# Attention scores on tiles of 64 rows by 128 columns, one head each, in a transformer block on one core

## The chip, the cores and the metric

The kernel runs on one core of one Trainium2 chip. A core has TensorE (PE in the profile, its weight loads as PEld), VectorE (DVE), ScalarE (ACT), GpSimd (POOL) and SyncE (SP), which work at the same time and wait for one another by semaphores; each takes its instructions in a fixed order. On-chip memory for operands has 128 partitions; products land in a memory of their own, PSUM. The metric is the time on the device in microseconds, the median of several runs. Before the change it is 972.0 us in three runs (971.28, 972.0, 973.32).

## The reference

One block: an adaptive layer norm, sliding-window attention, a second adaptive layer norm and a gated feed-forward net. S = 2048 positions, D = 512, 32 heads of 16 numbers each, a window of 256 positions, F = 1792.

```
mod = (silu(c) @ w_mod).reshape(...)            # sa, ca, ga, sb, cb, gb
h = layernorm(x) * (1 + ca) + sa
q, k, v = (h @ wqkv) split into 32 heads of 16
scores = q k^T * 16**-0.5,  kept where 0 <= i - j < 256, else -1e9
x = x + ga * ((softmax(scores) @ v) @ wo)
h = layernorm(x) * (1 + cb) + sb
x = x + gb * ((silu(h @ w1) * (h @ w3)) @ w2)
```

All inputs and the output are float32. The products with high demands are made from parts: a number is split into a part of reduced precision (type fp32r) and the rest, and three products (high-high, high-low, low-high) are added up.

## The kernel before

**Units.** Attention is cut into 32 units, 8 groups of four heads (g) by 4 blocks of 512 positions (b). A unit is made in three stages that run on different units at the same time: `unit_a` makes the queries and keys of a group for a block (12 products `pj`, line 451, then copies by ScalarE, two subtractions by GpSimd and six DMAs into the tile `ring`); `unit_b` makes the maximum of each row of scores; `unit_c` makes the probabilities and the output. In a unit there are four blocks of 128 queries (qb) or keys (j), and the four heads are two pairs (a) of two heads (hh).

**The tile ring** holds queries and keys with 16 x 3 = 48 rows a head, since each number stands in three parts. Before the change it has three planes of 96 rows each: the queries of two heads one above the other (rows interleaved), and for each of the two heads a plane of keys in which the rows of the other head are zero. So one score product (line 504, tile `mx`, 96 rows) takes the queries of both heads, and the zero rows of the keys drop the other head. Four more rows (96 to 99) hold the row maxima, in two parts for each head, against rows of ones and zeros in the keys; the score products for the probabilities (line 763, tile `st`, 100 rows) so subtract the maximum. `ring_fill` writes zeros and ones with memsets on GpSimd, five for each block.

**unit_b** makes 16 products `mx` a unit, up to 384 keys each. `top` (line 511, VectorE) adds a mask and takes the maximum from PSUM, then `parts`, a transpose on TensorE (line 526, `turn`), a copy on ScalarE and two DMAs (`rows`, line 535) bring the maxima into ring.

**unit_c** makes 16 products `st` a unit and masks them in a mode that is given for each key block and pair of heads in the string `MODE` (last three units: `MODL`). C: VectorE merges two blocks under a predicate (line 781), ScalarE takes the exponential, GpSimd splits the result again (line 791). P: masking by GpSimd in a side tile. D: VectorE adds the mask in PSUM (line 771), then one exponential. E: TensorE adds the mask by a further product with the identity (line 766), then one exponential. The value products (`pv`, line 739) use tiles of 128 rows by 32 columns: four heads side by side, each product recorded as two passes, all into one bank `po`; line 828 copies the finished bank and a DMA (`store`) writes it to memory. A key block's probabilities are used by up to three query blocks, so the last two key blocks of a unit give a second product in the next unit ("carry").

**Order of the work.** In attention the order on every engine is written out: each step of a unit has a time in the table `X`, in units of an eighth of a unit's length, and all steps of all units are sorted by those times. `pj`, `mx` and `tl`, `st`, `c`, `pv`, `o` are the times of the projections, of the score products and their maxima, of the probability scores, of what follows them, of the value products and of the copy and store of the output. A second table, `Y`, orders the first units, which run among the value projection (line 671). From the time `TS` = 232 on (the last three units) the steps have fixed planned times, `us(t)` with the paces `TW`, and a planner deals the output projection (line 1120) and the start of the feed-forward net (lines 1384 and 1478) around them, by estimated costs. PSUM: three banks for `mx`, three for `st`, one for `pj`, one for `po`.

Of the kernel before, what the change touches and what calls it, by code (L numbers as in the profile page):

```python
# [12 lines left out]
ALU = mybir.AluOpType  # L13
# [16 lines left out]
X = dict(oa=-1.228, ob=1.317, wqk=(-2.382, 3.131, 4.551), pj=(-1.966, -1.918, -1.881, -0.877, -0.359, -0.355,  # L30
         -0.265, 0.076, 1.497, 3.335, 3.917, 4.363), ev=(4.727, 5.775, 5.259), mix=(5.588, 6.021),
         row=(8.681, 8.806, 9.018), mx=(0.546, 0.669, 1.455, 2.0, 2.064, 2.307, 2.929, 2.957, 3.255, 4.081,
         4.688, 5.039, 6.139, 6.215, 6.787, 7.106), tl=(0.31, 0.576, 0.39, 0.716, 0.354, 0.742, 0.497, 1.151,
         0.762, 0.785, 0.491, 0.953, 0.338, 1.726, 1.317, 1.105), mr=(8.575, 8.773, 9.063, 9.269), st=(1.873,
         1.594, -2.503, 2.891, 0.05, 3.409, 2.644, 3.504, 4.618, 4.477, 4.419, 5.916, 5.311, 7.665, 6.691,
         6.671), c=(0.385, 0.805, 2.402, 0.573, 0.759, 1.126), pv=(4.115, 8.948, 9.091, 9.582, 3.792, 4.101),
         o=(9.93, 10.63), job=(-0.855, 2.493, 10.058))
# [9 lines left out]
MODL = 'CECECECE'  # L47
# [223 lines left out]
TW = (243.0, 1.7, 1.5)  # L271
# [31 lines left out]
def block_kernel(ctx: ExitStack, tc: tile.TileContext, x, wqk, wv, wo, w13, w2, c, wmod, out):  # L303
# [13 lines left out]
    def fill_odd():  # L317

        for hh in range(2):
            r = slice(64 * hh, 64 * hh + 64)  # L320
            nc.vector.tensor_reduce(
                out=odd[r], in_=ident[r].rearrange("p (c o) -> p c o", o=4)[:, :, 2 - 2 * hh:4 - 2 * hh],
                op=ALU.add, axis=mybir.AxisListType.XY)
# [80 lines left out]
    mskk = mskw[:, :2]  # L404
    nc.gpsimd.memset(mskk, 0.0)
    WIN = (dict(pattern=[[1, P]], base=0, channel_multiplier=-1, compare_op=ALU.is_ge, fill=NEG),
           dict(pattern=[[-1, P]], base=0, channel_multiplier=1, compare_op=ALU.is_gt, fill=NEG))
    for j in range(2):
        nc.gpsimd.affine_select(out=mskk[:, j], in_=mskk[:, j], **WIN[j])
    later = ap.tile([P, P], mybir.dt.uint8, name="later")  # L410
    mskr = ap.tile([P, 2, P], F32R, name="mskr")
# [1202 lines left out]
```

## Time and profile before

| what | value |
|---|---|
| median of three runs | 972.0 us (971.28 to 973.32) |
| profiled execution, span | 971.3 us |
| instructions | 17150 |
| TensorE busy | 942.4 us, 97% |
| TensorE weight loads | 717.5 us, 74% |
| VectorE busy | 734.9 us, 76% |
| ScalarE busy | 557.1 us, 57% |
| GpSimd busy | 538.2 us, 55% |
| score products for maxima, line 504 | 512, 154.9 us busy |
| score products for probabilities, line 763 | 512, 155.3 us busy |
| value products, line 739 | 1408 passes, 98.6 us busy |

The span is one execution, from the first to the last instruction; the profiled execution's own time is this span. Busy times are unions: two instructions of one engine that overlap count once. A product is recorded with the pipeline's tail, so its recorded length is more than the time for which it holds the array; that time is read from start to start. Roughly, the first 45 us are loading and the first layer norm, up to 97 us the value projection with the first units in it, up to 445 us attention in steady state, up to 530 us the last units and the output projection, and then the feed-forward net, which the change doesn't touch.

### The profile page before, as it was taken

How to read it: one execution, taken by the hardware profiler on the slowest of the kernel's cores; microseconds unless marked ns; L12 is line 12 of the kernel's file. 1: busy time of each engine (PE TensorE's matmuls, PEld its weight loads, DVE VectorE, ACT ScalarE, POOL GpSimd, SP SyncE). 2: the span in 40 equal slices, each digit the busy share in tenths (PEclk: the TensorE clock that was granted, in tenths of full speed). 3: DMA queues.
4: the chain of work that ended last, by engine and by line, in shares of the span. 5: the costliest groups of instructions: out<-in, count | busy, mean ns of one | idle time of the engine just before them, and what ended most of it. 6: DMA issues, size and time to landing. Idle time of an engine off the chain costs nothing.

```text
span 971.3 us, 17150 instructions
## 1 busy us (share of the span) xinstructions
PE 942.4 (97%) x5316; PEld 717.5 (74%) x5316; DVE 734.9 (76%) x2034; ACT 557.1 (57%) x1258; POOL 538.2 (55%) x740
## 2 busy tenths in 40 slices
PE   6999999999999999998998999999999999999998
PEld 3678777777767776775577888888887888888886
DVE  7575889998989998999278686666679766677545
ACT  3333878787878787876578843433456343433330
POOL 8321777787868786865546765337759332222320
PEclk9999999999999999999898999999999999999999
DMA  9521354444544444435795564467654433222102
GB/s 317 170 77 36 134 182 143 144 143 144 176 143 143 144 144 143 133 128 174 211 243 139 194 217 151 142 206 249 194 195 165 141 119 94 63 65 72 44 23 87
DMA packets 80672, 141.65 MB, mean 146 GB/s; under 512 B 9538, under 2 KB 22338, under 8 KB 80580
## 3 DMA queue, kind: packets, MB, share of 16 engines
q1 hardware_dynamic: 79860, 139.50, 44.6%
q10 hardware_dynamic: 720, 1.05, 0.3%
q8 instruction: 42, 0.69, 0.3%
q14 instruction: 50, 0.41, 0.1%
HBM read 85.72 MB, written 34.61 MB: 124 GB/s over the span
## 4 chain that ended last, share of the span: by engine, by line
PE 83%; POOL 5%; DVE 4%; DMA 3%; issue 2%; ACT 2%; SPq 1%; POOLq 0%; DVEq 0%; ACTq 0%
PE st L1384 13%; PE mx L1384 11%; PE pj L451 7%; PE mx L504 7%; PE mx L1478 7%; PE st L763 7%; PE st L1478 7%; PE po L739 6%; PE pj L1384 5%; PE st L671 3%; PE pj L1478 2%; PE mx L1120 2%; POOL pt L791 2%; PE st L1120 2%; POOL qk L469 2%
## 5 line engine op out<-in xcount | busy, mean ns | idle before, releaser
L511 DVE CUSTOM_DVE_ANT_0 junk<-mx,mskq 128x384 bf16<-128x384 f32 (+2 forms) x512 | 256.3, 527 | 28.8 <-PE mx L504 27.2
L504 PE MATMUL mx<-ring 96*128 96x384 f32 (+2 forms) x512 | 154.9, 340 | 6.0 <-DMA ring<-qk 2.4
L763 PE MATMUL st<-ring 100*128 100x384 f32 (+2 forms) x512 | 155.3, 345 | 2.2 <-ACT pt L784 1.2
L791 POOL TENSOR_SCALAR_AFFINE_SELECT pt<-pt 128x256 f32<-128x256 f32 x268 | 109.3, 411 | 63.1 <-ACT pt L784 52.5
L451 PE MATMUL pj<-hT,wq 128*128 128x512 f32 x384 | 136.2, 404 | 1.2 <-DVE wq L440 0.8
L504 PEld LDWEIGHTS mx<-ring 96*128 96x128 f32 x512 | 93.5, 189 | 39.7 <-DVE mt L511 25.8
L784 ACT ACTIVATE pt<-st 128x256 f32<-128x256 f32 x268 | 96.1, 386 | 41.8 <-DVE st L781 33.8
L763 PEld LDWEIGHTS st<-ring 100*128 100x128 f32 x512 | 95.5, 190 | 23.7 <-issue 8.4
L739 PE MATMUL po<-pt,vS 128*17 128x384 f32 (+2 forms) x1408 | 98.6, 398 | 1.7 <-POOL pt L791 1.0
L469 POOL TENSOR_TENSOR qk<-qkr,qk 128x512 fp32r<-128x512 f32 x64 | 83.3, 1302 | 27.6 <-ACT qkr L457 27.4
L976 POOL TENSOR_TENSOR w<-w,w 128x512 fp32r<-128x512 f32 (+2 forms) x36 | 59.8, 1679 | 62.0 <-ACT w L975 44.6
L1428 POOL TENSOR_TENSOR t<-t,t 128x512 f32<-128x512 f32 x28 | 39.7, 1418 | 93.5 <-DVE t L1416 91.7
L781 DVE COPY_PREDICATED st<-later,st 128x128 f32<-128x128 uint8 x268 | 72.2, 291 | 17.4 <-PE st L763 14.5
L451 PEld LDWEIGHTS pj<-hT,wq 128*128 128x128 f32 x384 | 71.4, 190 | 10.2 <-issue 1.7
L739 PEld LDWEIGHTS po<-pt,vS 128*17 128x17 f32 x1408 | 33.5, 98 | 48.4 <-issue 22.4
L1384 PE MATMUL st<-b,w 128*128 128x512 f32 x258 | 64.1, 390 | 0.0
L775 ACT ACTIVATE pt<-st 128x384 f32<-128x384 f32 (+2 forms) x128 | 52.7, 434 | 18.8 <-DVE st L771 12.4
L1416 DVE TENSOR_TENSOR t<-st,t 128x512 f32<-128x512 f32 x52 | 35.7, 686 | 36.4 <-PE st L1384 31.2
L808 POOL TENSOR_SCALAR_AFFINE_SELECT sm<-sm 128x256 f32<-128x256 f32 x109 | 42.1, 409 | 27.9 <-ACT sm L798 25.2
L1456 ACT ACTIVATE wq<-g 128x512 fp32r<-128x512 f32 x28 | 17.8, 634 | 67.5 <-PE st L1478 40.7
L1384 PE MATMUL mx<-b,w 128*128 128x512 f32 x222 | 56.0, 390 | 0.0
L1384 PEld LDWEIGHTS st<-b,w 128*128 128x128 f32 x258 | 48.4, 188 | 10.2
(270 smaller groups left out, 2083.1 us busy)
## 6 DMA issues: line engine op xcount, KB each, us to landing
ring<-qk SPq DMA_DIRECT2D x192, 128.0 KB
o_dr<-os SPq DMA_DIRECT2D x32, 256.0 KB
w<-wsum SPq DMA_DIRECT2D x14, 512.0 KB
w<-w2g SPq DMA_DIRECT2D x14, 512.0 KB
jb<-in_w SPq DMA_DIRECT2D x24, 256.0 KB
wraw<-in_w SPq DMA_DIRECT2D x7, 768.0 KB
w<-wraw SPq DMA_DIRECT2D x14, 384.0 KB
vS<-in_wmod SPq DMA_DIRECT2D x20, 256.0 KB
```

The costliest lines, as they stand in the source:

```text
L451: nc.tensor.matmul(v["ps"], WQ[g][w][:, n // 3], hTp(i, n // 3, b * BT, BT), start=(n == 0), stop=(n == 3 * KC - 1))
L469: nc.gpsimd.tensor_tensor(out=v[n], in0=v["raw"], in1=v[1].bitcast(F32), op=ALU.subtract)
L504: nc.tensor.matmul(v[i][:, :n], queries(NS, a, gq, 1), keys(NS, hh, a, k0, gq + 1 - k0), start=True, stop=True)
L511: nc.vector.tensor_tensor_reduce(out=junk[:, :n], in0=v[i][:, :n], in1=mskq[:, 3 * P - n:], scale=1.0, scalar=-3e38, op0=ALU.add, op1=ALU. ...
L739: nc.tensor.matmul(po[32 * i:32 * i + DH + 1, qb * P:(qb + nq) * P], vS[:, kb, 4 * g + i], pts[i // 2][:, i % 2, c0:c0 + nq], start=first, ...
L763: nc.tensor.matmul(ps[:, :nq], keys(NM, hh, a, kb, 1), queries(NM, a, kb, nq), start=True, stop=not plus)
L781: nc.vector.copy_predicated(ps[:, 0], later, ps[:, 2])
L784: nc.scalar.activation(held[u, j, a][:, hh, :2], v[j, a, hh][:, :2], AF.Exp, scale=SCALE)
L791: nc.gpsimd.affine_select(out=pt[:, :, 2 * m], in_=pt[:, :, 0], **w)
L976: sch.op(eng, lambda: on_eng(eng).tensor_tensor(out=lo(), in0=src(), in1=hi().bitcast(F32), op=ALU.subtract), tt(eng, n), key, kl + kh, kl ...
L1384: nc.tensor.matmul(ps(bk), WT[s, n][w][:, col], BB[t, k][r], start=start and c == 0, stop=stop and c == 5, skip_group_check=True)
L1478: nc.tensor.matmul(ps(bk), tiles[hk + (h,)][:, i * P:(i + 1) * P], w2_of(last, y, f), start=(m == 0), stop=(m == 5))
```

## The change

The score products lose their zero rows. `ring` has two planes, queries and keys, and each of the two heads of a pair has its own 64 partitions: head 0 in rows 0 to 47 (its maxima in rows 48 and 49), head 1 in rows 64 to 111 (112 and 113). A score product then takes 48 rows (`mx`) or 50 (`st`) at partition 0 or 64, which is a tile of 64 rows by 128 columns. `ring_fill` becomes one memset of ones on the key plane for each block. The six DMAs of a unit that bring queries and keys stay six; the maxima go by four DMAs of 8 rows each instead of two of 16.

`MODL` has D in place of E, so the kernel makes no mask products. The table `X` has new times for nearly all steps of a unit, `Y` stays, and `TW` has shorter paces for the last units. Since the first value product of a unit can now be any of them, `pv` sets its start flag for whichever comes first. The mask helpers and the layout of the weights on the host follow the new layout.

```diff
+X = dict(oa=-1.228, ob=1.317, wqk=(-2.382, 3.131, 4.551), pj=(-1.758, -1.34, -0.975, -0.96, -0.015, 0.978,
+         1.889, 1.977, 2.276, 2.306, 2.375, 4.26), ev=(5.435, 5.953, 5.299), mix=(6.004, 6.513), row=(8.597,
+         9.057, 9.768), mx=(5.756, 6.476, 3.618, 2.69, 4.383, 7.199, 1.554, 5.551, 2.012, 4.524, 3.665, 1.765,
+         0.572, 4.299, 0.072, 3.027), tl=(0.886, 0.662, 0.247, 0.419, 0.792, 0.139, 0.429, 0.474, 0.932,
+         1.296, 0.349, 1.035, 0.745, 0.051, 1.206, 0.64), mr=(7.551, 8.815, 8.912, 9.635), st=(-1.106, 1.276,
+         2.864, 1.977, -0.222, 2.887, 0.055, 2.604, 4.413, 4.273, 4.025, 4.982, 6.414, 6.945, 5.508, 5.686),
+         c=(0.438, 1.051, 2.778, 0.321, 0.685, 1.644), pv=(4.562, 7.607, 10.433, 10.471, 3.95, 3.335),
+         o=(10.779, 17.508), job=(-0.855, 2.493, 10.058))
...
-MODL = 'CECECECE'
+MODL = 'CDCDCDCD'
...
-TW = (243.0, 1.7, 1.5)
+TW = (243.0, 1.15, 1.1)
...
-    ring = ap.tile([P, 3, 2, S], F32R, name="ring")
-
-    NS, NM = 6 * DH, 6 * DH + 4
-
-    def queries(rows, a, b, n):
-        return ring[:rows, 1, a, b * P:(b + n) * P]
-
-    def keys(rows, hh, a, b, n):
-        return ring[:rows, 2 - 2 * hh, a, b * P:(b + n) * P]
+    ring = ap.tile([P, 2, 2, S], F32R, name="ring")
+
+    HP, NS, NM = P // 2, 3 * DH, 3 * DH + 2
+
+    def rg(x, rows, hh, a, t, n):
+        return ring[HP * hh:HP * hh + rows, x, a, t:t + n]
...
-    def ring_fill(b, hh):
-        k = ring.bitcast(F32)[:, 2 - 2 * hh, :, b * BT:(b + 1) * BT]
-        nc.gpsimd.memset(k[:NM] if hh == 0 else k[:NS], 0.0)
-        if hh:
-            nc.gpsimd.memset(k[NS:NM], 1.0)
-        nc.gpsimd.memset(k[NS:NS + 2], 1.0 - hh)
+    def ring_fill(b):
+        nc.gpsimd.memset(ring.bitcast(F32)[:, 1, :, b * BT:(b + 1) * BT], 1.0)
...
-                    rf[3 * hh + r:NS:6, 1 - hh:3 - hh, :, b * BT:(b + 1) * BT].rearrange(
+                    rf[HP * hh + r:HP * hh + NS:3, :, :, b * BT:(b + 1) * BT].rearrange(
                         "p x a t -> p (x a) t"),
-                    v[r].bitcast(F32)[64 * hh:64 * hh + 64, :])
+                    v[r].bitcast(F32)[HP * hh:HP * hh + HP, :])
...
-            nc.tensor.matmul(v[i][:, :n], queries(NS, a, gq, 1), keys(NS, hh, a, k0, gq + 1 - k0),
+            nc.tensor.matmul(v[i][:, :n], rg(0, NS, hh, a, gq * P, P), rg(1, NS, hh, a, k0 * P, n),
                              start=True, stop=True)
...
-            for a in range(2):
-                nc.sync.dma_start(ring.bitcast(F32)[NS:NM, 1, a, b * BT:(b + 1) * BT],
-                                  v["mT"][16 * a:16 * a + 16, :])
+            for n in range(4):
+                r = HP * (n // 2) + NS
+                nc.sync.dma_start(ring.bitcast(F32)[r:r + 2, 0, n % 2, b * BT:(b + 1) * BT],
+                                  v["mT"][8 * n:8 * n + 8, :])
...
-            nc.tensor.matmul(ps[:, :nq], keys(NM, hh, a, kb, 1), queries(NM, a, kb, nq),
+            nc.tensor.matmul(ps[:, :nq], rg(1, NM, hh, a, kb * P, P), rg(0, NM, hh, a, kb * P, nq * P),
                              start=True, stop=not plus)
...
+            first = "pv" not in v
+            v["pv"] = True
             if uu == u:
-                pv(kb, g, pts, j, 0, here, b == 0 and j == 0, j == 3)
-            elif nq > here:
-                pv(kb, g, pts, 0, here, nq - here, j == 2, False)
+                pv(kb, g, pts, j, 0, here, first)
+            else:
+                pv(kb, g, pts, 0, here, nq - here, first)
```

The times of X before are in the kernel above the functions: `pj=(-1.966, -1.918, -1.881, -0.877, -0.359, -0.355, -0.265, 0.076, 1.497, 3.335, 3.917, 4.363)`, `mx=(0.546, 0.669, 1.455, 2.0, 2.064, 2.307, 2.929, 2.957, 3.255, 4.081, 4.688, 5.039, 6.139, 6.215, 6.787, 7.106)`, `mr=(8.575, 8.773, 9.063, 9.269)`, `st=(1.873, 1.594, -2.503, 2.891, 0.05, 3.409, 2.644, 3.504, 4.618, 4.477, 4.419, 5.916, 5.311, 7.665, 6.691, 6.671)`, `pv=(4.115, 8.948, 9.091, 9.582, 3.792, 4.101)`, `o=(9.93, 10.63)`. The order of st and mx in these lists is by block, pair a and head hh (the last runs fastest).

More of the change, by code (lines that the diff above doesn't have):

```diff
@@ L692, in block_kernel @@
     at(h0 - 9, fill_masks)
[L693 to L695 removed]
+    at(h0 - 8.6, lambda: ring_fill(0))
+    at(h0 - 8.5, lambda: ring_fill(1))
     at(h0 - 3 + 1.5 * W["s"], fill_sc)
@@ L733, in block_kernel, with pv @@
     held = {}
-    def pv(kb, g, pts, qb, c0, nq, first, last):
+    def pv(kb, g, pts, qb, c0, nq, first):
         for i in range(4):
@@ L740, in pv @@
                              vS[:, kb, 4 * g + i], pts[i // 2][:, i % 2, c0:c0 + nq],
-                             start=first, stop=last, skip_group_check=True)
+                             start=first, stop=True, skip_group_check=True)
     def unit_c(u, t0, at):
```

34 lines of the change are left out of this document (10 added, 24 removed).

## The prediction

> **What bounds the kernel now.** I began with the busy share of each engine and then cut the span into its stages (stretch in us, its length, then busy us and instructions of TensorE, its weight loads, VectorE, ScalarE and GpSimd, the granted clock, DMA share and rate).
>
> ```profile
> PE 942.4 (97%) x5316; PEld 717.5 (74%) x5316; DVE 734.9 (76%) x2034; ACT 557.1 (57%) x1258; POOL 538.2 (55%) x740
> ```
>
> ```profile
> 45.00:97.00 52.00, 50.53 (x238) 40.22 (x239) 35.99 (x110) 19.35 (x34) 12.32 (x12) 1.00 0.22 70
> 125.00:445.00 320.00, 313.82 (x2379) 226.65 (x2379) 289.29 (x1233) 252.01 (x714) 239.49 (x439) 1.00 0.44 146
> 445.00:485.00 40.00, 35.26 (x224) 20.68 (x223) 22.93 (x68) 22.92 (x59) 19.12 (x29) 0.87 0.68 205
> 485.00:515.00 30.00, 30.00 (x152) 23.95 (x152) 20.85 (x42) 22.40 (x42) 17.03 (x13) 1.00 0.97 240
> ```
>
> The change touches the first three rows and the join to the fourth. In the head (45 to 97: value projection and first scores) TensorE is 97% busy. In the steady stage (125 to 445) it is 98% busy, but VectorE follows at 90%. From 445 to 485, the last units, TensorE has 4.7 us of idle time and a granted clock of 0.87.
>
> The copies of the finished output bank give the length of a unit: 29 up to 444.6 us, so (444.6 - 109.9) / 28 = 11.95 us; three more to 488.1, so 14.5 us each at the end.
>
> ```profile
> L828 ACT ACTIVATE os<-po x29: 597/597/601, 109.9 to 444.6; 128x512 f32<-128x512 f32 x29
> ...
> L828 ACT ACTIVATE os<-po x32: 579/597/601, 109.9 to 488.1; 128x512 f32<-128x512 f32 x32
> ```
>
> VectorE's floor is 289.29 / 320 x 11.95 = 10.80 us a unit. So the steady stage can give back 1.15 us a unit and no more, however short TensorE's work gets. The waits of this stage (total us, times, longest) show how close the two are: each waits for the other about 21 us in 320.
>
> ```profile
> DVE junk L511 <- PE mx L504: 21.5, 45, 1.9
> ...
> PEld mx L504 <- DVE mt L511: 20.1, 42, 0.6
> ```
>
> **What TensorE's work costs.** Its order of time in one unit (start, length with the pipeline's tail, line, tile, count), and the weight loads at the end of it:
>
> ```profile
> 202.11 0.52 PE L763 MATMUL st<-ring 100*128 100x384 f32 x2
> 202.47 0.34 PE L504 MATMUL mx<-ring 96*128 96x384 f32 x1
> 202.65 0.40 PE L451 MATMUL pj<-hT,wq 128*128 128x512 f32 x1
> 202.89 0.34 PE L504 MATMUL mx<-ring 96*128 96x384 f32 x1
> 203.16 1.60 PE L739 MATMUL po<-pt,vS 128*17 128x384 f32 x24
> 204.68 0.45 PE L763 MATMUL st<-ring 100*128 100x384 f32 x1
> 204.97 0.34 PE L504 MATMUL mx<-ring 96*128 96x384 f32 x1
> 205.14 0.34 PE L763 MATMUL st<-ring 100*128 100x384 f32 x1
> ```
>
> ```profile
> 204.68 0.19 PEld L763 LDWEIGHTS st<-ring 100*128 100x128 f32 x1 [0.21 <-issue]
> 204.79 0.19 PEld L504 LDWEIGHTS mx<-ring 96*128 96x128 f32 x1
> ```
>
> Read start to start. A score product holds TensorE for (202.65 - 202.11) / 3 = 0.18 us, a projection (pj) for 0.24. Where the array goes from 128-column products to the 17-column tiles of po, the score before them takes 203.16 - 202.89 = 0.27: 0.09 too long. Back again, the first score takes 204.97 - 204.68 = 0.29: 0.11 too long, which is the time from its weight load to the next (204.79 - 204.68); elsewhere a load runs under the product before it. I read an **edge** between tilings as a drain of 0.09, plus 0.11 where the next product loads 128 columns; that leaving a po group drains like entering one is an assumption.
>
> That tiles of the array do run together is seen in po: 512 products of 501 ns fit into 56.9 us of busy time, 4.5 deep.
>
> ```profile
> L739 PE MATMUL po<-pt,vS 128*17 128x384 f32 x512 | 56.9, 501 | 0.3 <-POOL pt L791 0.3
> ```
>
> **The change part by part.** The times in X, taken modulo 8, give the order on TensorE in a steady unit. s and m are score products for probabilities (st) and for maxima (mx) with the head's number, J a projection, T the transpose, V a value product of four tiles.
>
> ```
> before: s0 m0 J m1 V V V s1 m0 s0 m0 T J s0 J m0 s1 J m1 m0 s1 s1 m1 V V V m0 m1 s0 s1 m0 s0 J J J s0 m1 s0 J s1 m0 m1 J J J s1 s0 J m0 m1 s1
> after:  s0 m1 J J J J J s1 m0 m0 s1 T V V s1 s0 m0 s1 J m1 m0 V V m1 s0 s1 m1 s0 V m0 m0 s1 J J s0 m1 s1 m0 J J m1 s0 J m1 s0 s1 m0 V J s0 m1
> ```
>
> *Pairs.* Head 0 will lie in rows 0 to 47, head 1 in rows 64 to 111. If two neighbours of different heads run side by side, the 32 scores of a unit (nine runs, the last joining the first) take 17 places instead of 32: 15 x 0.18 = 2.70 us less a unit. The nearest row for this is po's overlap.
>
> *Value groups.* Four groups of V instead of two. One group costs 0.09 going in and 0.09 + 0.11 coming out, 0.29: two more are +0.58 a unit.
>
> *Edges between scores and the rest.* Before, scores and J have the same tiling (202.65 above: no gap, 0.18). After, a unit has 12 such edges (T counted with J). No row shows the price x of an edge to row tiles. Bounds: 0 (score to J now) and 0.20 (po's 0.09 + 0.11). I take 0.20, since po is the only change of tiling that the trace has. It is +2.40.
>
> [...]
>
> Steady sum: -2.70 + 0.58 + 2.40 = +0.28 us a unit, over 28 units **+8**. In general a unit changes by -2.12 + 12x, but never below VectorE's floor.
>
> *The head.* Here the order is Y's, which stays. Its 32 score products stand singly among 128-row products, so none finds a partner, and each gets two edges.
>
> ```profile
> 45.00:97.00 52.00, 10.60 (x32) 6.01 (x32) 1.00 0.22 70
> ```
>
> ```profile
> 82.01 0.34 PE L504 MATMUL mx<-ring 96*128 96x384 f32 x1
> 82.19 0.40 PE L671 MATMUL st<-wvl,hT 128*128 128x512 f32 x1
> 82.42 0.63 PE L671 MATMUL st<-wvh,hT 128*128 128x512 f32 x2
> ```
>
> The first of these fences holds line 504 alone in the head, 32 products; the second one of them with no gap around it (0.18, 0.23). 32 x 2 x 0.20 = 12.8, less the stretch's idle 52 - 50.53 = 1.5: **+11**.
>
> *The last three units.* Mode E becomes D: 24 mask products go (20 of 256 columns, 4 of 128), at 0.18 per 384 columns 20 x 0.12 + 4 x 0.06 = 2.6 us, and 24 additions come to VectorE, about 0.4 us each (the mean below), 9 us where it has 17 idle in 40.
>
> ```profile
> L766 PE MATMUL st<-mskr,identr 128*128 128x256 f32 x20 | 5.9, 293 | 0.0
> ...
> L766 PE MATMUL st<-mskr,identr 128*128 128x128 f32 x4 | 1.0, 250 | 0.0
> ```
>
> ```profile
> L771 DVE TENSOR_TENSOR st<-st,mskr 128x256 f32<-128x256 f32 (+1 forms) x94 | 32.7, 368 | 0.0
> ```
>
> TensorE is not the bound there, so neither counts in full. What counts is how densely the fixed steps are set among the planner's: with TW the planner puts the end of attention at 38.4 of its us instead of 43.1. The three units now take 3 x (14.5 - 11.95) = 7.7 us more than steady ones. I give back two thirds, **-5**, with ends +5 (edges around output projections, additions ahead of the exponentials) and -10 (all of it and the mask products).
>
> *What I cost at nothing.* The filling of ring is one memset a block instead of five; those of about 1 us lie on GpSimd, 76% idle in the head. The split maxima go back in four DMAs instead of two: two more issues of 0.68 us a unit on SP, which waits 77.7 us in this stage at that line alone.
>
> ```profile
> L535 SPq DMA_DIRECT2D ring<-mT x53: 659/677/727, 124.4 to 435.1; - x53
> ```
>
> ```profile
> SPq L535 <- ACT pt L784: 77.7, 20, 5.4
> ```
>
> Queued behind them on SP are the rows of the next projection; st reads the maxima about four of X's eight steps later, 6 us. The store of a unit's output moves from 10.63 to 17.508, past the next unit's rows on SP; in the last unit it is about 7 planned us later, covered by the output projections of the other three blocks, which fill the row from 485 to 515.
>
> **Sum**: 8 + 11 - 5 = +14 on the profiled 971.3; the median 972.0 stands 0.7 above it: **986 us**.
>
> **Rivals.**
> *Edges to row tiles are free (x = 0); the time goes down.* TensorE falls to 11.95 - 2.12 = 9.8 a unit, VectorE's 10.80 becomes the bound; at 96% busy a unit takes 11.2: -0.75 x 28 = -21, head 0, end -5: **946**. For it: the present 96-row and 128-row products join without a gap. Against: po's edges. It decides at -59.4 + 336x (steady) + 64x - 1.5 (head) - 5 = 0, x = 0.165: below that the kernel gets faster.
> *Half an edge (x = 0.11, load exposed, no drain).* TensorE 11.95 - 2.12 + 1.32 = 11.15 beside VectorE's 10.80, say 11.4: -15; head 7 - 1.5 = +5.5; end -5: **957**. [...]
> *The pairs don't run together*, the change doesn't do what it says: 2.70 x 28 = 76 more than the sum, **1061**. For it: the overlap seen is of column tiles only.
>
> **How the numbers follow.** Forecast 0.53 (inside it the end leaves about 0.06 faster and 0.03 the same), free edges 0.18, half an edge 0.17 (0.01 of it the same), no pairs 0.06, the rest 0.06 above the forecast. Within 0.2% is about what this kernel's runs can tell from no change (971.28 to 973.32). Faster 0.40, same 0.04, slower 0.56. Own range of the forecast: 975 to 998 (end -10 to +5, steady stage +/-6). Taken down to 947 for the two faster rivals and up to 1000 it leaves out the pairless case and the lowest of the free edges.
>
> **What would show it.** In the steady stage: scores of different heads starting within some ns of each other; the score before a J taking 0.27 instead of 0.18 and the first after it 0.29; a unit of 12.2 us with VectorE near 88%. In the head: every single mx with both edges, the stage 11 us longer. The prediction is wrong if scores and J still join at 0.18, if VectorE stands at 95% or more, or if the end after 445 gains over 10 us because the output projections' loads start earlier.

## The result and the profile after

The changed kernel takes 1064.0 us (median of four runs, 1057.8 to 1079.3) against 972.7 before: 1.091 times as long (95% interval 1.087 to 1.095). Executions of a kernel with row tiles differ by up to 5.4% (unpaired, 1261.1 to 1329.8 us), so ratios are taken over the shorter ones and need not be those of the medians, while the profiled execution is a longer one for five kernels below (old paces, early maxima with old paces, pairs in the head, both unpaired ones). The prediction was 986, slower, with a range up to 1000: the sign is right, the size is not, and the time lies outside the range.

The first line of the page and the same stretches of the work in the kernel after (stretch, length, busy us and instructions of TensorE, its weight loads, VectorE, ScalarE and GpSimd, granted clock, DMA share and rate):

```profile
PE 995.4 (94%) x5292; PEld 646.6 (61%) x5292; DVE 756.6 (72%) x2058; ACT 555.5 (53%) x1258; POOL 522.0 (49%) x724
```

```profile
45.00:107.00 62.00, 61.75 (x242) 38.65 (x238) 36.10 (x111) 19.48 (x34) 9.27 (x8) 1.00 0.18 58
...
135.00:490.00 355.00, 343.75 (x2375) 165.07 (x2375) 297.01 (x1228) 248.90 (x715) 240.85 (x440) 0.94 0.40 131
490.00:535.00 45.00, 35.88 (x238) 14.40 (x236) 30.77 (x103) 22.83 (x60) 11.88 (x27) 0.68 0.46 138
535.00:565.00 30.00, 18.19 (x63) 13.39 (x63) 14.00 (x22) 14.26 (x25) 22.86 (x15) 0.74 0.88 239
565.00:580.00 15.00, 11.26 (x32) 8.30 (x33) 12.44 (x18) 6.65 (x14) 5.90 (x4) 0.61 0.60 174
580.00:615.00 35.00, 26.86 (x119) 21.03 (x118) 21.96 (x41) 23.72 (x44) 17.01 (x14) 0.90 0.29 98
```

The head, which the value projection ends, needs 62 us for the same work instead of 52, TensorE still full. In the steady stage the granted clock is 0.94 on average; before it was 1.00. And from 535 to 615, where the output projection had TensorE full before, TensorE works only 56 of 80 us.

Three marks give the account: the copy of the first unit's output, that of unit 28, and the last product of the output projection (line 1120 before, 1113 after). The rows for the copies after and the last output projections before and after:

```profile
L821 ACT ACTIVATE os<-po x29: 597/598/601, 123.2 to 496.6; 128x512 f32<-128x512 f32 x29
```

```profile
L1120 PE MATMUL mx<-wo,o x96: 387/389/776, 482.9 to 536.9; 128*128 128x512 f32 x96
```

```profile
L1113 PE MATMUL st<-wo,o x24: 387/389/504, 611.7 to 623.0; 128*128 128x512 f32 x24
```

| stretch | before | after | difference | predicted |
|---|---|---|---|---|
| start to the first unit's copy | 109.9 | 123.2 | +13.3 | +11 |
| first copy to that of unit 28 | 334.7 | 373.4 | +38.7 | +8 |
| from there to the last output projection | 92.4 | 126.5 | +34.1 | -5 |
| from there to the end | 434.4 | 433.1 | -1.3 | 0 |
| span | 971.3 | 1056.1 | +84.8 | +14 |

**Pairs and edges** are both there. TensorE in order of time, first the head, then a steady unit at full clock:

```profile
92.74 0.39 PE L664 MATMUL st<-wvl,hT 128*128 128x512 f32 x1
92.97 0.40 PE L664 MATMUL st<-wvh,hT 128*128 128x512 f32 x1
93.30 0.43 PE L496 MATMUL mx<-ring 48*128 48x384 f32 x1
93.66 0.50 PE L664 MATMUL st<-wvh,hT 128*128 128x512 f32 x1
94.00 0.40 PE L664 MATMUL st<-wvl,hT 128*128 128x512 f32 x1
```

```profile
359.39 0.44 PE L754 MATMUL st<-ring 50*128 50x384 f32 x1
359.55 0.39 PE L496 MATMUL mx<-ring 48*128 48x384 f32 x1
359.87 0.73 PE L443 MATMUL pj<-hT,wq 128*128 128x512 f32 x2
360.53 0.44 PE L754 MATMUL st<-ring 50*128 50x384 f32 x1
360.54 0.55 PE L496 MATMUL mx<-ring 48*128 48x384 f32 x2
360.82 0.34 PE L754 MATMUL st<-ring 50*128 50x384 f32 x1
361.09 0.74 PE L443 MATMUL pj<-hT,wq 128*128 128x512 f32 x2
```

A lone mx in the head: the product before it holds TensorE for 0.33 us instead of 0.23, mx itself 0.36 instead of 0.18, the one after it 0.34 instead of 0.23. That is 0.10 + 0.18 + 0.11 = 0.39 for two edges. At 360.53 and 360.54 an st and an mx of different heads start within 0.01 us, the next two follow at 360.8, so four scores take 361.09 - 360.53 = 0.56 us with both edges instead of 0.72. Over the whole steady stage, 12.1 pairs of scores a unit start within 0.01 us of each other, where the prediction counted 15, and TensorE changes 11.7 times a unit between scores and 128-column products, where it counted 12.

**The clock** is the new thing. Two stretches of the steady stage, and one between them for comparison:

```profile
345.00:480.00 135.00, 130.99 (x947) 63.22 (x948) 118.69 (x492) 98.47 (x284) 95.14 (x174) 1.00 0.41 134
215.00:228.00 13.00, 13.00 (x46) 5.51 (x46) 7.52 (x31) 5.73 (x17) 7.12 (x14) 0.50 0.36 122
327.50:341.00 13.50, 13.50 (x48) 6.01 (x40) 6.79 (x28) 5.14 (x16) 6.00 (x11) 0.50 0.33 116
```

At granted clock 0.50 TensorE is busy all the time and gets through 3.5 instructions a us instead of 7.0. There are four such stretches in the steady stage, 50 us in all (none before in the profiled execution). The four units that hold them take 14.7 to 18.7 us, 69.2 together; the other 24 take 12.7 on average. So of the +38.7, 69.2 - 4 x 11.95 = 21.4 lie in the units with half clock and 24 x 0.72 = 17.3 in the others.

### The profile page after: what moved, and what is told of

The parts are those of the page before. It is cut to its first block, busy times and chain, and to the rows that moved or that the text cites. A ratio compares the mean times of both kernels' runs of the same rounds, so it can differ in the third digit from the quotient of the medians.

```text
span 1056.1 us, 17283 instructions
## 1 busy us (share of the span) xinstructions
PE 995.4 (94%) x5292; PEld 646.6 (61%) x5292; DVE 756.6 (72%) x2058; ACT 555.5 (53%) x1258; POOL 522.0 (49%) x724
## 4 chain that ended last, share of the span: by engine, by line
PE 75%; DVE 7%; DMA 6%; ACT 4%; issue 3%; POOL 2%; SPq 2%; POOLq 0%; ACTq 0%; DVEq 0%
PE mx L1377 10%; PE pj L443 10%; PE st L1377 9%; PE po L730 6%; PE mx L1471 6%; PE mx L496 6%; PE st L754 6%; PE st L1471 6%; PE st L664 4%; PE pj L1377 3%; DMA ring<-mT 3%; PE pj L1471 2%; SPq L528 2%; PE st L1113 1%; ACT pt L766 1%
## 5 line engine op out<-in xcount | busy, mean ns | idle before, releaser
L496 PE MATMUL mx<-ring 48*128 48x384 f32 (+2 forms) x512 | 169.5, 407 | 4.9 <-DVE mt L503 2.6
L754 PE MATMUL st<-ring 50*128 50x384 f32 (+2 forms) x512 | 162.1, 418 | 12.6 <-DMA ring<-mT 7.3
L443 PE MATMUL pj<-hT,wq 128*128 128x512 f32 x384 | 149.0, 464 | 1.3 <-ACT wq L428 0.9
L496 PEld LDWEIGHTS mx<-ring 48*128 48x128 f32 x512 | 82.5, 195 | 72.4 <-DVE mt L503 35.4
L754 PEld LDWEIGHTS st<-ring 50*128 50x128 f32 x512 | 81.0, 198 | 67.0 <-ACT pt L775 18.8
L730 PE MATMUL po<-pt,vS 128*17 128x384 f32 (+2 forms) x1408 | 110.9, 420 | 0.0
L1409 DVE TENSOR_TENSOR t<-mx,t 128x512 f32<-128x512 f32 x55 | 37.8, 688 | 38.2 <-PE mx L1377 34.2
L1377 PE MATMUL mx<-b,w 128*128 128x512 f32 x258 | 64.2, 397 | 0.0
L1377 PEld LDWEIGHTS mx<-b,w 128*128 128x128 f32 x258 | 49.7, 193 | 10.6
L762 DVE TENSOR_TENSOR st<-st,mskr 128x256 f32<-128x256 f32 (+1 forms) x128 | 46.7, 377 | 13.0 <-PE st L754 8.8
```

Of the source, the lines that this page charges most:

```text
L443: nc.tensor.matmul(v["ps"], WQ[g][w][:, n // 3], hTp(i, n // 3, b * BT, BT), start=(n == 0), stop=(n == 3 * KC - 1))
L496: nc.tensor.matmul(v[i][:, :n], rg(0, NS, hh, a, gq * P, P), rg(1, NS, hh, a, k0 * P, n), start=True, stop=True)
L730: nc.tensor.matmul(po[32 * i:32 * i + DH + 1, qb * P:(qb + nq) * P], vS[:, kb, 4 * g + i], pts[i // 2][:, i % 2, c0:c0 + nq], start=first, ...
L754: nc.tensor.matmul(ps[:, :nq], rg(1, NM, hh, a, kb * P, P), rg(0, NM, hh, a, kb * P, nq * P), start=True, stop=not plus)
L1377: nc.tensor.matmul(ps(bk), WT[s, n][w][:, col], BB[t, k][r], start=start and c == 0, stop=stop and c == 5, skip_group_check=True)
L1409: return nc.vector.tensor_add(o, x, y)
```

## The experiments

Times are medians; the ratio to the kernel before, run on the same chip at the same time, has its 95% interval. "Half clock" is the time at granted clock 0.5 between the first unit's copy and that of unit 28; "end" is from unit 28's copy to the last output projection; both are from the one profiled execution.

| run | us | ratio | steady | half clock | end |
|---|---|---|---|---|---|
| before | 972.7 | 1 | 334.7 | 0 | 92.4 |
| after | 1064.0 | 1.091 (1.087-1.095) | 373.4 | 50 | 126.5 |
| paces alone | 992.4 | 1.019 (1.016-1.022) | 334.4 | 0 | 112.2 |
| after, old paces | 1058.2 | 1.076 (1.066-1.085) | 395.0 | 106 | 103.8 |
| tiles alone | 1030.9 | 1.058 (1.056-1.061) | 370.5 | 17 | 101.9 |
| positions alone | 1015.3 | 1.043 (1.040-1.046) | 355.6 | 7 | 97.9 |
| after, early maxima | 1048.4 | 1.075 (1.067-1.083) | 374.4 | 48 | 111.6 |
| the same, old paces | 1054.1 | 1.074 (1.068-1.079) | 392.2 | 90 | 98.9 |
| the same, pairs in the head | 1043.7 | 1.060 (1.054-1.066) | 388.7 | 76 | 99.0 |
| late store alone | 1002.9 | 1.034 (1.031-1.037) | 346.8 | 7 | 112.4 |
| after, early store | 1063.0 | 1.095 (1.089-1.100) | 392.4 | 93 | 110.9 |
| after, early store, old paces | 1057.5 | 1.091 (1.084-1.097) | 374.0 | 51 | 100.3 |
| after, projections grouped | 1074.3 | 1.105 (1.103-1.107) | 388.7 | 83 | 124.9 |
| no mask products alone | 995.4 | 1.024 (1.022-1.026) | 336.5 | 3 | 112.9 |
| before, fewer projections | 968.5 | 0.994 (0.991-0.996) | 330.2 | 3 | 93.8 |
| mask in the score step | 976.9 | 1.004 (1.002-1.006) | 333.9 | 3 | 95.6 |
| after, unpaired | 1311.6 | none on record (1261 to 1330 us) | 634.8 | 635 | 128.3 |
| unpaired and grouped | 1122.9 | 1.155 (1.150-1.159) | 451.0 | 219 | 127.4 |

### One part at a time

**Paces alone.**

```diff
-TW = (243.0, 1.7, 1.5)
+TW = (243.0, 1.15, 1.1)
```

> The kernel before with only the shorter paces TW of the change. Theory (the planner, told that the last units are short, puts the loads and splits of the output projection behind them, and TensorE then stands still): the time from the cut of unit 28 to the last output projection grows from 92 to about 120 us and the kernel takes about 1000 us. Rival (the loss at the end comes from the tiles and the slower clock, the paces are harmless): 972, within 5.

As the theory had it in kind, with somewhat less than its 120 and 1000 us: the last three units do get shorter (11.6, 11.4 and 10.1 us instead of 14.5, 13.6 and 15.5), but the end is 19.8 us longer. TensorE stands still there; these are the windows of that stretch:

```profile
474.50:489.50 15.00, 13.99 (x80) 10.46 (x79) 5.22 (x12) 7.40 (x17) 8.02 (x6) 1.00 0.93 295
489.50:504.50 15.00, 5.13 (x11) 2.72 (x11) 8.69 (x13) 11.07 (x20) 11.34 (x8) 0.62 0.67 175
```

**The changed kernel with the old paces.**

```diff
-TW = (243.0, 1.15, 1.1)
+TW = (243.0, 1.7, 1.5)
```

> The changed kernel with the old paces TW. Theory: the end falls from 126 back to 95 to 100 us, the rest stays: about 1034 us. Rival (paces harmless): 1064, within 5.

The end falls by 22.7 us as expected, but the median only by 6, and by the ratios (1.091 and 1.076) the kernel gains 15: in the profiled execution half clock takes 106 us of the steady stage instead of 50. The changed kernel's executions took 1058 to 1079 us and those of this one 1041 to 1063, so the forecast of 1034 was missed, and the rival's (1064 within 5, paces harmless) too, since the end did move.

**Tiles alone.** The changed kernel with the whole of X, TW and MODL of the kernel before.

```diff
-MODL = 'CDCDCDCD'
+MODL = 'CECECECE'
-TW = (243.0, 1.15, 1.1)
+TW = (243.0, 1.7, 1.5)
```

> The 64-row tiles alone: positions X, paces TW and MODL are those of the kernel before. Theory (each change between 64-row scores and 128-row products costs 0.2 us, pairs run together): head +10 to +13; in a steady unit 16 such edges at 0.2 and about 11 pairs at 0.18, +1.2 us, so +34; a slower clock where TensorE waits: 1020 to 1045 us. Rival (edges to row tiles cost nothing, the new positions are what costs): 972 or less.

1031: inside the expectation, and stage by stage: head +12.0, steady stage +35.8 (expected +34). Five single stretches of 3.4 us, 17 us in all, are at half clock: the four units longer than 14.5 us take 14.9 on average, the other 24 take 12.95, which is 1.0 above the 11.95 of before where edges and pairs alone were to give 1.2. The trace has the counts of the expectation: 15.7 edges and 10.5 pairs a unit. That row tiles cost nothing at their edges is refuted.

**Positions alone.** The kernel before with X of the change and the flags of `pv` and `mt` that any order needs.

```diff
-            if i == 0:
+            if "mt" not in v:
...
+            first = "pv" not in v
+            v["pv"] = True
             if uu == u:
-                pv(kb, g, pts, j, 0, here, b == 0 and j == 0, j == 3)
+                pv(kb, g, pts, j, 0, here, first)
```

> The kernel before (96-row tiles with zero rows) with the new positions X alone; paces and MODL are the old ones. Theory (the positions cost only two more groups of value products a unit, 0.58 us, and some waits for maxima that arrive late): 972 + 16 to 25, so 988 to 997, granted clock as before. Rival (the positions are the main cost of the steady stage, since the maxima arrive after the scores that need them): 1010 or more, and a unit of 13.3 us.

The theory missed; the rival had the time (1010 or more) but not the unit of 13.3 us. The unit is 12.70 us (median 12.4), so +21 in the steady stage where 16 was the price of two more groups of value products; 3.5 us go in the head, 5.5 in the end, and 10 behind the last output projection. This X holds the late store too, which was costed at nothing. Tiles and positions don't add up: +35.8 and +20.9 alone in the steady stage, +38.7 together.

**Late store alone.**

```diff
-         o=(9.93, 10.63), job=(-0.855, 2.493, 10.058))
+         o=(9.93, 17.508), job=(-0.855, 2.493, 10.058))
```

> The kernel before with the store of a unit's output at 17.508 instead of 10.63, nothing else. What was costed at nothing: 972 within 3. Rival (the last units' stores hold up the output projection's loads): 5 to 15 us slower, all of it after the cut of unit 28.

Costed at nothing, and it takes 32 us: 12 in the steady stage, 20 in the end. The rival, 5 to 15 us and all of it at the end, missed as well. The waits of the steady stage name the first part: ScalarE's copy of the finished bank waits for the DMA that stores the copy before, since there is one buffer for it.

```profile
ACT os L828 <- DMA o_dr<-os: 14.8, 7, 3.6
```

In the changed kernel the copy moved as well (to 10.779), and this wait is 0.3 us in its steady stage. Nor does the part at the end carry over as it is: with the new positions and the old paces the same late store leaves the end 5.5 us longer than before (positions alone).

**No mask products alone.**

```diff
-MODL = 'CECECECE'
+MODL = 'CDCDCDCD'
```

> The kernel before with D in place of E in the last three units, nothing else. Theory (TensorE isn't the bound there, VectorE has room): 972 within 3. Rival (the additions hold up the exponentials of the last units): 3 to 8 us slower, all after the cut of unit 28.

24 us slower, three times the upper end of the rival. The end shows one long wait of TensorE for ScalarE, in a product of the feed-forward net that was dealt ahead of output projections:

```profile
PE mx L1384 <- ACT t L1419: 10.6, 1, 10.6
```

The two traces, compared by line and tile in the order of each engine, differ on every engine: a diff has 1590 lines for TensorE's products, 314 for VectorE, 196 for ScalarE, 66 for GpSimd and 126 for SyncE, for 24 products that became 24 additions. So:

**Mask in the score step.** The kernel before; VectorE adds the mask, but inside the step that the planner already had.

```diff
-                             start=True, stop=not plus)
+                             start=True, stop=True)
             if plus:
-                nc.tensor.matmul(ps[:, bl], identr, mskr[:, :nm], start=False, stop=True)
+                nc.vector.tensor_tensor(out=ps[:, bl], in0=ps[:, bl], in1=mskk[:, :nm], op=ALU.add)
```

> The kernel before with the mask of the last three units added by VectorE instead of TensorE, as in the run without mask products, but written into the score step itself, so that the planner sees the same steps and deals the same order: ScalarE's, GpSimd's and SyncE's orders are those of the kernel before. Theory (the loss without mask products came from the new deal of everything after the steady stage, with its keys tuned to the old one): 972 within 5. Rival (the additions on VectorE, or the clock that the mask products had kept up, are the loss): 990 or more.

976.9, 0.4% slower, the end 95.6, as the theory had it. The same diff now has 24 lines for TensorE, the products that went, 24 for VectorE, the additions that came, and none for the other engines. So the same additions cost 4 us in the old order and 24 when the planner deals anew. The stretch in which the two differ, first with the new deal, then with the old:

```profile
530.00:550.00 20.00, 7.13 (x18) 4.52 (x17) 15.84 (x24) 10.70 (x21) 12.32 (x10) 0.57 0.05 20
```

```profile
530.00:550.00 20.00, 19.80 (x93) 16.48 (x94) 14.53 (x33) 17.79 (x35) 12.68 (x10) 1.00 0.41 145
```

Paces, store time and mask mode are all inputs of the same planner, and each one alone leaves the end at 112 to 113 us. For the mask mode the new deal is shown to be the cause. Paces alone and the late store alone change the order as much (1834 and 1876 lines for TensorE), but what the new order costs there was not separated from the edit itself.

### Putting the end back in the changed kernel

```diff
-         o=(10.779, 17.508), job=(-0.855, 2.493, 10.058))
+         o=(10.779, 11.4), job=(-0.855, 2.493, 10.058))
```

> The changed kernel with the store of a unit's output at 11.4 instead of 17.508, nothing else. Theory (the late store holds up the loads of the output projection after the last units; it was costed at nothing): from the cut of unit 28 to the last output projection 126 falls to 105 to 110 us, the steady stage stays, the whole about 1045. Rival (with the new paces the loads are behind the units anyway): 126 stays within 3, 1064 within 8.

> The changed kernel with the early store and the old paces TW. Theory (store and paces together are the loss at the end, the tiles add about 5): that stretch 95 to 100 us, the whole about 1030. Rival (tiles and half clock hold the end up too): 104 or more, as with the old paces alone.

The early store gives 15.6 us at the end, near the theory; with the old paces as well the end is 100.3, so these two account for 26 of the 34 us. Of the store's part, 3.5 us are left once the paces are old (103.8 against 100.3). The whole times, forecast at 1045 and 1030, hardly move in the median (1063.0 and 1057.5). In the first, what the end gives back is taken by more half clock in the steady stage (93 us). The second ran from 1040 to 1065 us at a granted clock of 0.950 to 0.920 over the span; the profiled execution is its shortest and keeps what the end gave back.

### The head

The maxima scores of the first units in pairs, on the kernel with early maxima and old paces:

```diff
-         ev=(4.991, 4.614, 4.813), mix=(5.389, 5.444), row=(5.416, 5.471, 6.776), mx=(0.0, 0.5, 1.0, 1.5,
-         2.0, 2.5, 3.0, 3.5, 4.0, 4.5, 5.0, 5.5, 6.0, 6.5, 7.0, 7.5), tl=(0.402, 0.402, 0.402, 0.402, 0.402,
+         ev=(4.991, 4.614, 4.813), mix=(5.389, 5.444), row=(5.416, 5.471, 6.776), mx=(0.0, 0.0, 1.0, 1.0,
+         2.0, 2.0, 3.0, 3.0, 4.0, 4.0, 5.0, 5.0, 6.0, 6.0, 7.0, 7.0), tl=(0.402, 0.402, 0.402, 0.402, 0.402,
```

> As the run before it, with the maxima scores of the first two units placed in pairs of both heads (Y's mx: 0, 0, 1, 1, ... instead of 0, 0.5, 1, 1.5, ...). Theory (edges of 0.2 us between row tiles and 128-row products; pairs run together): 32 edges and 16 places of 0.18 us less, so the last value projection ends near 97 us instead of 105.6, and the whole is 7 to 9 us shorter. Rival (the head is longer for another reason, such as VectorE): no change of more than 2 us.

The last value projection is at 99.9 instead of 105.3 us (rows below; first the run without pairs): 5.4 us of the expected 8.6. All 16 pairs do start together in the trace. That supports edges and places as what the head loses, and speaks against the rival. The whole is 10 us shorter in the median, but its four executions range from 1024 to 1075 us.

```profile
L664 PE MATMUL st<-wvh,hT x128: 387/396/505, 20.6 to 105.3; 128*128 128x512 f32 x128
```

```profile
L664 PE MATMUL st<-wvh,hT x128: 387/396/503, 19.6 to 99.9; 128*128 128x512 f32 x128
```

### The half clock

In the changed kernel each of the four falls of the clock comes within 3 us after st of a unit of block 0 has waited for the DMA of the maxima; here the clock falls at 214.8. The theory was that these waits bring it about. The same waits stand at 163.8, 382.1 and 433.3 us too, with no fall behind them.

```profile
213.29 0.44 PE L496 MATMUL mx<-ring 48*128 48x384 f32 x1 [0.20 <-DVE mt L503]
214.08 0.41 PE L754 MATMUL st<-ring 50*128 50x384 f32 x1 [0.35 <-DMA ring<-mT]
214.76 0.78 PE L754 MATMUL st<-ring 50*128 50x384 f32 x2 [0.28 <-DMA ring<-mT]
```

**Early maxima.**

```diff
-         1.296, 0.349, 1.035, 0.745, 0.051, 1.206, 0.64), mr=(7.551, 8.815, 8.912, 9.635), st=(-1.106, 1.276,
+         1.296, 0.349, 1.035, 0.745, 0.051, 1.206, 0.64), mr=(7.551, 7.883, 8.0, 8.3), st=(-1.106, 1.276,
```

> The changed kernel with the transpose of the maxima, its copy and its DMAs placed earlier (mr from 8.815, 8.912, 9.635 to 7.883, 8.0, 8.3), nothing else. Theory (in the units of block 0, which have no carried value products, the probability scores reach TensorE before the maxima have landed; each of these waits, where it falls into one window of the clock, halves the granted clock for 13.6 us): no waits for the maxima's DMAs in the steady stage, no halved clock there, steady stage from 373 to about 352 us, all in all about 1042. Rival (the clock falls because row-tiled products keep too little of the array busy): as many stretches of half clock as before, 1064 within 10.

> The kernel with the earlier maxima and, besides, the old paces TW. Theory: the paces are worth 20 us at the end also here: about 1020 us, from the cut of unit 28 to the last output projection about 104 us. Rival (the paces only matter while the clock is low): within 5 us of the run with the earlier maxima.

The waits are gone (one is left, where the kernel after has 24 in 355 us), but 48 us of half clock remain, at other places; with the old paces 90. The theory falls: the waits can choose the moment, they are not the cause. The whole is 16 us shorter, but the gain lies at the end (111.6 against 126.5), not in the steady stage. The medians of the two runs are 6 us apart, just outside the 5 of the second one's rival, though the end does get 12.7 us shorter.

**Fewer projections**, on the kernel before; the products of the projection with the low parts are left out from the fourth unit on, so this kernel computes less.

```diff
-        for n in range(3 * KC):
+        for n in range(0, 3 * KC, 1 if u < 3 else 3):
             at(t0 + y["pj"][n], lambda n=n: product(n), "product")
```

> The kernel before with 4 instead of 12 projection products in each unit from the fourth on (the products with the low parts are left out), no row tiles, no new edges. It takes 8 x 0.235 = 1.9 us off TensorE's work in a unit, about as much as the paired scores do. Theory (the clock falls because TensorE has less to do than VectorE lets through, whatever the tiles): stretches of half clock in the steady stage, 20 us of them or more, and a unit near 11.9 on average or worse. Rival (the half clock comes from row tiles and their drains): full clock through the steady stage and a unit of 10.8 to 11.3, so 20 to 30 us faster than before.

Neither. The clock stays up but for one stretch of 3.4 us, so taking this much off TensorE's work does not halve it. And the unit hardly gets shorter: (439.8 - 109.6) / 28 = 11.79 us, 0.16 less for 1.9 us of TensorE's work.

```profile
L828 ACT ACTIVATE os<-po x29: 597/599/600, 109.6 to 439.8; 128x512 f32<-128x512 f32 x29
```

**Fewer edges.** On the changed kernel, projections in two groups of six:

```diff
-X = dict(oa=-1.228, ob=1.317, wqk=(-2.382, 3.131, 4.551), pj=(-1.758, -1.34, -0.975, -0.96, -0.015, 0.978,
-         1.889, 1.977, 2.276, 2.306, 2.375, 4.26), ev=(5.435, 5.953, 5.299), mix=(6.004, 6.513), row=(8.597,
+X = dict(oa=-1.228, ob=1.317, wqk=(-2.382, 3.131, 4.551), pj=(-0.98, -0.976, -0.972, -0.968, -0.964, -0.96,
+         1.889, 1.977, 2.276, 2.306, 2.375, 2.38), ev=(5.435, 5.953, 5.299), mix=(6.004, 6.513), row=(8.597,
```

> The changed kernel with the projections of a unit in two groups of six instead of six groups (pj only), so 5 edges between scores and 128-row products a unit instead of 12. Theory (an edge is TensorE's time lost, and drains keep the clock low once it has fallen): a unit at full clock takes 11.4 to 12.0 us instead of 12.6 to 12.8, half clock ends after one or two windows of 3.4 us; steady stage 330 to 345 instead of 373. Rival (TensorE then only waits for VectorE and its clock falls more often): 12.4 or more at full clock and at least 40 us of half clock.

The rival holds: 12.3 us and more at full clock, and 83 us of half clock. Seven edges less are 1.4 us less of TensorE's work a unit, and the unit at full clock gets at most 0.4 shorter: as in the run before, work taken off TensorE returns little. (The trace has 4.9 edges and also fewer pairs, 9.0 a unit.) Of the theory one part is seen: a stretch of half clock now mostly lasts 3.4 or 6.8 us, but there are fourteen of them.

**Unpaired**, the changed kernel with the heads of the maxima scores exchanged in the order, and then also grouped:

```diff
-            qb, a, hh = i // 4, i // 2 % 2, i % 2
+            qb, a, hh = i // 4, i // 2 % 2, 1 - i % 2
```

> The changed kernel with the two heads of the maxima scores exchanged in the order (hh becomes 1 - i % 2), so that in a steady unit most neighbours belong to the same head: 27 places of 0.18 us instead of 17, the same edges, the same row tiles. Theory (pairs are worth 0.18 each, and the half clock comes from pairs and drains together leaving the array idle too long): a unit of about 14 us at full clock, half clock in the steady stage under 15 us, the whole 1070 to 1090. Rival (row tiles as such bring the half clock): 40 us of half clock or more, and units of 18 us and longer as before.

> The changed kernel with the heads exchanged as in the run without pairs and the projections in two groups of six, so 5 edges between scores and 128-row products instead of 12. Theory (products that fill only 48 or 50 of 128 rows, one after the other, keep the clock halved, whatever the drains): 300 us of half clock or more in the steady stage. Rival (the drains at the edges keep it halved): half clock in stretches of 3 to 14 us, less than 120 us in all, and a steady stage under 450 us.

The theory of the first was wrong by a wide margin, and its rival's signs came: the clock falls at 114 us and does not come back before 800. Windows of that stretch:

```profile
200.00:300.00 100.00, 99.96 (x396) 49.43 (x389) 51.23 (x208) 44.93 (x122) 42.15 (x77) 0.50 0.23 75
300.00:400.00 100.00, 99.98 (x382) 49.06 (x383) 49.34 (x199) 41.76 (x115) 40.17 (x75) 0.50 0.24 81
```

TensorE is busy without a gap by these rows and is granted half the clock; a unit takes 22.9 us. With 5 instead of 12 edges between scores and projections half clock falls from 635 to 219 us: neither forecast of the second run, which asked for over 300 or under 120. Side by side (pairs: scores that start within 0.02 us of each other; edges: changes between scores and 128-column products; both counted in the trace, per steady unit; the last column has every execution, over the whole span):

| kernel | pairs | edges | half clock in the steady stage, us | granted clock |
|---|---|---|---|---|
| positions alone (96 rows) | none | none | 7 | 0.981 to 0.984 |
| tiles alone | 10.5 | 15.7 | 17 | 0.972 to 0.975 |
| after | 12.3 | 11.7 | 50 | 0.923 to 0.949 |
| after, projections grouped | 9.0 | 4.9 | 83 | 0.932 |
| unpaired | 6.5 | 11.7 | 635 | 0.728 to 0.780 |
| unpaired and grouped | 5.1 | 4.9 | 219 | 0.869 to 0.899 |

In these runs only kernels with row tiles have long half clock: the same positions with 96 rows have 7 us of it. Row tiles are not enough: tiles alone, with the most edges, has 17 us in the old order, at a granted clock of 0.972 to 0.975. With few pairs, fewer edges help much (635 to 219 us); with more pairs they show no gain (50 to 83 us). So the counts of pairs and edges don't settle it, and the order of the steps has a part.

What comes before a fall can be read in the traces of the kernels before and after. The shortest stretch of half clock in the kernel before is 3.41 us (455.84 to 459.25). I cut both steady stages into pieces of that length, counted from the changes of the clock, and take the fill of a piece to be the share of it in which at least one product streams its columns, estimated at 0.16 us for 384 (359.39 to 359.55 above); drains, waits and tails then count as empty. The changed kernel has 94 pieces at full clock, with a median of 56%; those in front of its four falls are filled to 34, 46, 38 and 34%. But eight others are filled to 38 to 45% with no fall behind them, among them the three that end at 163.6, 382.1 and 433.3, next to the waits named above. Of the 97 pieces of the kernel before, with a median of 73%, two are filled to 28 and 41%, again with no fall. So each of the four falls comes after a sparse piece, but a sparse piece does not bring one by itself. By the same reckoning the median is 73% with positions alone, 60% with fewer projections and 57% with tiles alone (7, 3 and 17 us of half clock). Where products run in pairs and edges leave gaps, the pieces are emptier throughout; that this brings the falls was not shown. What ends half clock stays open: in tiles alone each of the five stretches lasted 3.4 us, while in the unpaired kernel one lasted from 114 to 800 us.

## Why the prediction was wrong

**Pairs (-2.70 a unit): right in kind, too large.** Scores of different heads start within 0.01 us of each other, but 12.1 pairs a unit do so instead of 15, which by the same 0.18 us is -2.2. The rival without pairs gave 1061, next to the measured 1064, but its mechanism didn't happen; the number meets by accident.

**Edges (x = 0.20): right.** No row of the kernel before showed x for row tiles; in the changed kernel an edge was measured as neither free nor 0.11. The bound taken from po's edges is what row tiles cost, 0.39 for two in the head; with tiles alone, 27 lone scores between projections hold TensorE for 0.37 us (median) instead of 0.18, and the projection behind scores for 0.34 instead of 0.23. The head came out at +10.0 up to the last value projection (105.7 against 95.7) and +13.3 to the first copy, predicted +11. Tiles alone gave +35.8 in the steady stage where the same prices gave +34, some 8 us of it being what the four long units take beyond the others.

**The steady stage (+8): mis-sized, measured +38.7.** The sum took the granted clock as 1.00 throughout; 21.4 us lie in the units with half clock. The other units are 0.72 us longer, not 0.28. With the counts that the trace has (12.1 pairs, 1.75 more groups of value products, 11.7 edges) the sum's own prices give -2.18 + 0.51 + 2.34 = +0.67, so the three missing pairs are most of this part. The sum also took TensorE's work as if TensorE alone set the unit, and the waits of TensorE's weight loads for VectorE grew (first the row for the merge before, then in the kernel after for the maximum, the merge and the addition):

```profile
PEld mx L504 <- DVE st L781: 1.8, 2, 1.1
```

```profile
PEld mx L496 <- DVE mt L503: 26.9, 66, 1.3
...
PEld mx L496 <- DVE st L772: 17.0, 33, 1.2
...
PEld mx L496 <- DVE st L762: 7.6, 31, 0.3
```

That is 51.5 us in 355; before, it was 20.1 in 320 for the maximum and 1.8 for the merge. No run separates what waits and lost pairs cost; they can be two sides of one thing, since a score that waits starts away from its partner. VectorE itself is busy 84% of the stage, where 88% was forecast. "The steady stage can give back 1.15 us a unit" was too much as well: in the old order 1.9 us less work on TensorE gave 0.16. So the first two rivals, which count on VectorE's 10.80 as the floor, would probably have missed even with free edges; for the new order no run shows it.

**The last units (-5): wrong in sign, measured +34.1.** This is the step that failed most: 39 of the 71 us between sum and span. Its direction for the units themselves was right (39.0 us for the three, before 43.5). What it left out is that TW, the store time and MODL are inputs of the planner that deals all work after 232, on every engine, with keys that fit one deal. Each of the three alone costs about 20 us at the end, and they don't add up; in the changed kernel, taking back paces and store gives 26 of the 34 us. That the new deal is what costs is shown for MODL alone. The forecast's own range was also added up unevenly: an end of -10 to +5 instead of -5 and 6 us either way give 975 to 1002, not 998.

**What was costed at nothing.** The store: "covered by the output projections" was false, 32 us alone, 15.6 at the end of the changed kernel. The mask products: neither TensorE nor VectorE was the bound, true within 4 us, and yet 24 us, of which 20 come from the new deal. The maxima: they don't land 6 us before st reads them; st waits for them 24 times, mostly in units of block 0, 7.0 us in 355. The filling of ring and the two more DMAs were not tested alone.

What would have been seen beforehand: the prediction named the clock of 0.87 in the last units as a fact of the stage and did not ask what would lower it elsewhere. Nor did it ask which other steps the planner would move when its inputs change.

## What to carry to other kernels

The smaller product was not the cheaper one here, since it changed the tiling of the array: a lone score of 48 rows cost the head 0.39 us more than one of 96. Count the changes of tiling in the order of the work (here 0.20 us each) before counting the pairs (0.18 us each), and look first at places where the order can't be changed, like the head here (+13.3 us). When TensorE is given smaller products, read the granted clock stage by stage; busy time didn't show it here (99.96 of 100 us busy at 0.50). Where a planner orders the rest of the program, an edit to its inputs is an edit to everything behind it: hold the deal fixed to measure the edit itself.

## What the runs showed of the hardware that I had not expected

- In the unpaired kernel TensorE was busy in 99.96 of 100 us (200 to 300) at granted clock 0.50, and the clock stayed down from 114 to 800 us, with products of 48 and 50 rows and changes of tiling between them. In the changed kernel the four stretches of half clock that begin in the steady stage lasted 13.7, 10.2, 13.7 and 13.7 us; with row tiles in the old order (tiles alone) five lasted 3.4 us each.
- In the changed kernel, products streamed for 34 to 46% of the 3.41 us before each of the four falls, against a median of 56%; eight more pieces filled to 38 to 45% had no fall behind them.
- A change between 64-row tiles and 128-row products cost 0.20 us (0.39 for the two of a lone score in the head of the changed kernel), the same as one between 32-column tiles and 128-column products (0.09 + 0.11 in the kernel before). Where 128 columns are loaded after the change, the next load came 0.11 us later both times (93.66 to 93.77 after, 204.68 to 204.79 before).
- Two products in row tiles of different heads start within 0.01 us of each other (360.53 and 360.54 in the changed kernel) and take the place of one, four scores 0.56 us with both edges instead of 0.72: in the steady stage 12.1 pairs a unit.
